# Where prepared weight halves are stored, decoded and fetched in a three-layer chain

## The chip, the cores and the metric

The program runs on one core of a Trainium2 chip, in one launch. The metric is the device time of that core in microseconds (us), lower is better; three runs of the kernel before gave a median of 1521.45 us (1521.2 to 1522.31). The profile shows one execution of its own, which took 1519.77 us, of which the span from its first to its last instruction is 1518.0 us.

The engines named below: PE (TensorE) multiplies matrices, DVE (VectorE), ACT (ScalarE) and POOL (GpSimd) work element by element, and SP (SyncE) issues every DMA of this program from one queue. Each engine executes its own list of instructions in the order in which it was written; between engines there are only waits on semaphores.

## The reference, cut to what matters

```python
attn_out = attention(q, k, v)            # 2 x 8 heads x 768 tokens x 64, state decays per head
x = attn_out.transpose(0, 2, 1, 3).reshape(1536, 512)
# mixture of 8 experts, every token goes through all of them
P = sinkhorn(exp(x @ w_gate - max))      # 8 rounds, 1536 x 8
for e in range(8):                       # w1[e] 512 x 1024, w2[e] 1024 x 512
    out += P[:, e:e+1] * (maximum(x @ w1[e], 0) @ w2[e])
x = out
# a last layer with 2048 hidden columns and float64 weights
h = x @ w_in
out = (maximum(h, 0) + alpha * minimum(h, 0)) @ w_out
```

All three layers are wanted to float32 accuracy. The kernel gets it by splitting each operand into a high half that TensorE takes as it is and a low half that holds the rest, and by adding three products (high x high, high x low, low x high).

## The kernel before

After the attention the program is 20 phases in a row (`PHASES`): phases 0 to 7 are the eight experts on the first 768 tokens, phases 8 to 15 the eight experts on the other 768, and phases 16 to 19 the last layer, two for each half of the tokens. Each phase has a first layer and a second layer.

**First layer.** It is done by blocks: `order` (L1000 to L1003) lists 28 block products, four column blocks j = 0 to 3 with seven products p = 1 to 7 each, and `product` (L606) issues six matmuls of 384 columns for each. The bookkeeping that joins the products is in `after` (L654): after product 1, ACT copies the bank A into the bank B (L669), and PE needs that copy before product 6 may add to B. After product 5, ACT copies D into d. After product 6, DVE writes E = B + d (L672), and after product 7 it writes D = B + d (L685); both must have read B before PE adds the next product to it. `block` turns the finished banks into the high and low halves of the hidden layer (`hh` by ACT, `hl` by DVE).

**Second layer, phases 0 to 7.** `layer2` (L697) goes through six token pieces t; in one piece PE does 24 matmuls of 512 columns, in two halves, keys `t0a` and `t0`, up to `t5a` and `t5`. After each piece DVE adds it to `total` (L720). **Second layer, phases 8 to 15.** It is done by blocks again, from halves that were prepared earlier and lie in DRAM (`c2`): `fast2` has 28 steps u = 0 to 27, keys 0 to 27, and `ws_load` (L771) fetches the prepared pieces.

**What is put between.** The table `hooks` holds, for a key, the functions that are called right after the PE work of that key has been written; `at(ph, key, ...)` adds to it, and functions of one key stand in the order in which they were added. So a hook decides after which PE work an instruction stands in the list of its own engine, and nothing else. Four kinds of work are put in by hooks and concern the change:

- *Units of prepared halves.* 32 units (`prep_load`, `prep_sums`, `prep_low`, `prep_store`, L154 to L184) take a block of `w2`, form four sums on DVE (L168), convert them on ACT into the tile `pw` (L170), take the rest on DVE (L177), and store `pw` (1024 KB) to `c2` by SP (L184). The tile `pw` has one buffer: ACT may write the next unit only when the store of the unit before has landed. In phases 1 to 6 there are five units per phase, in phase 7 two.
- *Decoding.* 32 pieces of the float64 weights are read (`rd`), turned into float32 (two DVE steps, one ACT step `ex` at L578, three DVE steps) and stored (`wd`) by `decode` (L572), which then asks for the next `rd`. Phases 1 to 6 take two pieces each, phases 8 to 15 two or three.
- *Token pieces.* 14 pieces of the tokens of the last layer are split by POOL and ACT into the tile `xs` and stored to `xc` (`x_keep`, L228), in phases 9 to 14, and fetched (`x_fetch`) in the second layer of phase 15.
- *Transposes.* `turn` (L849) and `spread_turn` (L837) put a few transposes on PE, with a copy by ACT and a store.

Of the kernel before, what the change touches and what calls it, by code (L numbers as in the profile page):

```python
# [8 lines left out]
F32 = mybir.dt.float32  # L9
# [35 lines left out]
def tile_kernel(ctx, tc, qkT, kv, ctab, w_gate, w1, w2, w_in, w_out, alpha, out):  # L45
# [182 lines left out]
    def x_keep(g, k):  # L228
        b1, b2 = x_load(g, k)
        b11, b12 = b1[:, 0:HT], b1[:, HT:S]  # L230
        b21, b22 = b2[:, 0:HT], b2[:, HT:S]
        ta, tb = (
            tmp.tile([128, 1024], F32, tag="u" + w, name=f"t{w}{g}_{k}")[:, 0:2 * HT].rearrange("p (a b) -> p a b", a=2)
            for w in "ab"
        )
        eng = nc.gpsimd
        src = {B11: b11, T1: ta[:, 0], T2: ta[:, 1], B21: b21, T3: tb[:, 0], B22: b22, T4: tb[:, 1]}
        terms = {T1: (b12, b11), T2: (b22, ta[:, 0]), T3: (b12, b22), T4: (b21, ta[:, 1])}
        held = {}

        def make(q):
# [36 lines left out]
    with tc.manual_schedule():  # L278
# [292 lines left out]

        def decode(u, then):  # L572
            kind, j, half = u
            t = rd.pop(u)
            lo, hi = (t.rearrange("p (f w) -> p f w", w=2)[:, :, q] for q in range(2))
            ex = tp.tile([128, 512], U32, tag="tmp", name=f"ex{kind}_{j}_{half}")
            nc.vector.tensor_scalar(out=ex, in0=hi, scalar1=0x7FF00000, scalar2=None, op0=ALU.bitwise_and)  # L577
            nc.scalar.activation(out=ex, in_=ex, func=AF.Relu, bias=ebias, scale=8.0)  # L578
            a = tp.tile([128, 512], U32, tag="tmp", name=f"a{kind}_{j}_{half}")
            nc.vector.tensor_scalar(  # L580
                out=a, in0=hi, scalar1=0x000FFFFF, scalar2=0x00100000, op0=ALU.bitwise_and, op1=ALU.bitwise_or
            )
            q = a.bitcast(F32)
            nc.vector.scalar_tensor_tensor(out=q, in0=lo, scalar=2.0 ** -32, in1=a, op0=ALU.mult, op1=ALU.add)
            nc.vector.scalar_tensor_tensor(
                out=q, in0=q, scalar=2.0 ** -20, in1=ex.bitcast(F32), op0=ALU.mult, op1=ALU.mult
            )
            nc.vector.scalar_tensor_tensor(
                out=a, in0=hi, scalar=0x80000000, in1=a, op0=ALU.bitwise_and, op1=ALU.bitwise_or
            )  # L590
            nc.sync.dma_start(out=wd[kind][j][:, 512 * half:512 * half + 512], in_=q)
            if then:
                decode_load(then)

# [278 lines left out]
        def decode_at(ph, keys):  # L873
            for key in keys:
                if todo:
                    u = todo.pop(0)
                    at(ph, key, lambda u=u, then=todo[0] if todo else None: decode(u, then))
# [12 lines left out]

        xk = []
        for ph in range(len(PHASES)):
# [25 lines left out]
            if 1 <= ph <= 6:  # L918
                decode_at(ph, ("t0a", "t5a"))
                prep_at(ph, (0, 2), (1, 1))  # L920
                for t in range(1, 5):
                    prep_at(ph, f"t{t}a", f"t{t}")
            elif ph == 7:
                prep_at(ph, (0, 2), (1, 1))
                prep_at(ph, (1, 2), (2, 1))
            elif fast:
                decode_at(ph, ((0, 6), (2, 5)) if ph % 2 else ((0, 6), (1, 1), (2, 5)))
                if ph > E + 1:
# [39 lines left out]
        for a, (key, later) in enumerate((("t3", (0, 1)), ("t4", (0, 1)), ("t4", (0, 5)), ("t5", (0, 5)))):  # L968
# [3 lines left out]
        at(1, (0, 7), spread_turn)  # L972
        for a in range(KD):
# [25 lines left out]

        order = [(0, 1), (0, 5), (0, 6), (0, 2), (0, 7)]  # L1000
        for j in range(1, NJ):
            order += [(j, 1), (j, 5), (j - 1, 4), (j, 6), (j - 1, 3), (j, 2), (j, 7)]
        order += [(NJ - 1, 3), (NJ - 1, 4)]  # L1003
        for ph in range(len(PHASES)):
# [93 lines left out]
```

## Time and profile before

| | |
|---|---|
| median of three runs | 1521.45 us |
| the profiled execution | 1519.77 us, span 1518.0 us |
| PE busy | 1329.6 us (88%), 7179 matmuls |
| DVE, ACT, POOL busy | 938.1, 631.9, 401.2 us |
| DMA | 296.79 MB, 58.0% of the 16 engines' time |
| mean granted clock of TensorE | 0.940 |

A busy PE is not a PE at its best: matmuls are pipelined, and the profile also counts those that run at the lower of the two clock levels. So the table is read with the length of each phase beside it: the phases from 1 on take between 60 and 100 us, for nearly the same number of matmuls.

### The profile page before, as it was taken

To read this page: it belongs to the slowest core of one execution; us is meant where nothing else is said; L and a number is where in the kernel's file an instruction comes from. 1 tells how busy PE (TensorE), PEld (TensorE's weight loads), DVE (VectorE), ACT (ScalarE), POOL (GpSimd) and SP (SyncE) were. 2 spreads that over 40 slices of the span, in tenths; PEclk is the share of its full clock that TensorE was granted. 3 is DMA by queue.
4 is the path that set the end of the run, shared out by engine and by line. 5 is a ranking of instruction groups with operands and counts; after the bars stand their busy time and mean duration, and the time that the engine had idled before them with its cause. 6 is when DMAs were issued, how large, how long until landed. Compare 5 with 4: busy or idle time off the path is not lost.

```text
span 1518.0 us, 19409 instructions
## 1 busy us (share of the span) xinstructions
PE 1329.6 (88%) x7179; PEld 1229.0 (81%) x7179; DVE 938.1 (62%) x1562; ACT 631.9 (42%) x1129; POOL 401.2 (26%) x335
## 2 busy tenths in 40 slices
PE   9899959687795949659898989988898999999998
PEld 6798849586785849558797979988798998898897
DVE  5666655655555646546576757867577786377552
ACT  2544324241423324234444444634445454364551
POOL 3843203040312204031001212030320227153440
PEclk9999979899897979879999989999999999999999
DMA  9453857567484856647575747675675756132211
GB/s 367 142 194 124 278 195 239 197 210 261 161 298 153 276 202 215 207 156 229 200 265 186 263 142 265 199 261 193 215 231 166 264 212 216 62 112 83 98 42 42
DMA packets 123070, 296.79 MB, mean 196 GB/s; under 512 B 11440, under 2 KB 43744, under 8 KB 118880
## 3 DMA queue, kind: packets, MB, share of 16 engines
q1 hardware_dynamic: 122976, 295.56, 58.0%
q8 instruction: 56, 0.92, 0.2%
q14 instruction: 38, 0.31, 0.1%
HBM read 198.24 MB, written 97.28 MB: 195 GB/s over the span
## 4 chain that ended last, share of the span: by engine, by line
PE 55%; DMA 20%; DVE 10%; ACT 7%; issue 4%; POOL 2%; SPq 1%; ACTq 0%; DVEq 0%
DMA c<-pw 11%; PE B L187 6%; PE B L188 6%; PE B L189 6%; PE o L187 5%; PE o L189 5%; PE o L188 5%; PE A L187 3%; PE A L189 3%; PE A L188 3%; DMA xc<-xs 3%; PE E L187 2%; PE E L188 2%; PE E L189 2%; DVE pw L177 2%
## 5 line engine op out<-in xcount | busy, mean ns | idle before, releaser
L113 POOL TENSOR_TENSOR raw<-raw 128x256 f32<-128x256 f32 x108 | 91.0, 853 | 236.0 <-DVE raw L113 91.1
L170 ACT ACTIVATE pw<-pr 128x1024 fp32r<-128x1024 f32 x32 | 33.9, 1058 | 266.7 <-DMA c<-pw 210.7
L762 DVE TENSOR_TENSOR hs<-b,hs 128x768 fp32r<-128x768 f32 x96 | 93.7, 976 | 52.2 <-ACT hs L761 52.2
L794 POOL TENSOR_TENSOR total<-total,t 128x384 f32<-128x384 f32 x56 | 60.4, 1104 | 237.0 <-DVE t L790 237.0
L761 ACT ACTIVATE hs<-b 128x768 fp32r<-128x768 f32 x96 | 80.9, 843 | 34.0 <-DVE b L736 16.1
L672 DVE TENSOR_TENSOR E<-B,d 128x384 f32<-128x384 f32 x80 | 45.0, 563 | 62.6 <-PE B L189 55.6
L669 ACT ACTIVATE B<-A 128x384 f32<-128x384 f32 x80 | 38.6, 483 | 92.6 <-PE A L189 90.7
L177 DVE TENSOR_TENSOR pw<-pr,pw 128x512 fp32r<-128x512 f32 x64 | 52.6, 863 | 27.9 <-ACT pw L170 27.9
L187 PE MATMUL B<-hs,ws 128*128 128x384 f32 x192 | 64.3, 335 | 2.2 <-DMA ws<-c 2.2
L189 PE MATMUL B<-hs,ws 128*128 128x384 f32 x192 | 64.2, 334 | 0.0
L188 PE MATMUL B<-hs,ws 128*128 128x384 f32 x192 | 64.1, 334 | 0.0
L168 DVE TENSOR_TENSOR pr<-pr 128x256 f32<-128x256 f32 x128 | 57.1, 446 | 4.5 <-DMA pr<-in_w_dram 1.2
L246 POOL TENSOR_TENSOR xs<-b,xs 128x384 fp32r<-128x384 f32 x6 | 7.1, 1188 | 174.3 <-ACT xs L245 174.3
L720 DVE SCALAR_TENSOR_TENSOR total<-o,P,total 128x512 f32<-128x512 f32 x42 | 31.4, 747 | 27.6 <-PE o L189 27.6
L578 ACT ACTIVATE ex<-ex,ebias 128x512 uint32<-128x512 uint32 x32 | 23.2, 724 | 58.6 <-DVE ex L577 58.6
L685 DVE TENSOR_TENSOR D<-B,d 128x384 f32<-128x384 f32 x48 | 27.1, 565 | 31.9 <-PE B L189 31.9
L628 DVE SCALAR_TENSOR_TENSOR hl<-D,hh 128x384 fp32r<-128x384 f32 x32 | 17.8, 557 | 43.8 <-ACT hh L627 41.6
L113 DVE TENSOR_TENSOR raw<-raw 128x256 f32<-128x256 f32 x84 | 44.0, 541 | 1.4
L187 PE MATMUL A<-hs,ws 128*128 128x384 f32 x128 | 42.9, 335 | 0.0
L188 PE MATMUL A<-hs,ws 128*128 128x384 f32 x128 | 42.8, 335 | 0.0
L189 PE MATMUL A<-hs,ws 128*128 128x384 f32 x128 | 42.8, 334 | 0.0
L714 ACT ACTIVATE total<-o 128x512 f32<-128x512 f32 x18 | 10.8, 598 | 69.7 <-PE o L189 69.7
(3435 smaller groups left out, 4745.3 us busy)
## 6 DMA issues: line engine op xcount, KB each, us to landing
ws<-c SPq DMA_DIRECT2D x112, 512.0 KB, 6.0
raw<-in_w_dram SPq DMA_DIRECT2D x64, 512.0 KB, 4.1
c<-pw SPq DMA_DIRECT2D x32, 1024.0 KB, 6.0
c<-raw SPq DMA_DIRECT2D x32, 512.0 KB, 5.2
pr<-in_w_dram SPq DMA_DIRECT2D x32, 512.0 KB, 6.9
raw<-c SPq DMA_DIRECT2D x32, 512.0 KB, 6.3
raw<-wd SPq DMA_DIRECT2D x32, 512.0 KB, 3.6
raw<-in_w_dram SPq DMA_DIRECT2D x32, 384.0 KB, 5.2
```

Source lines behind the costliest of these rows:

```text
L113: eng.tensor_tensor(out=out, in0=in0, in1=in1, op=op)
L168: nc.vector.tensor_tensor(out=out, in0=in0, in1=in1, op=op)
L170: nc.scalar.activation(out=ph2[i][:, :, 0, :], in_=pr[i].rearrange("p (a b) -> p a b", a=4), func=AF.Copy)
L177: nc.vector.tensor_tensor(out=ph2[i][:, a:a + 2, 1, :], in0=v[:, a:a + 2], in1=ph2[i][:, a:a + 2, 0, :].bitcast(F32), op=ALU.subtract,)
L187: nc.tensor.matmul(ps, ah, bh, start=first, stop=False, skip_group_check=True)
L188: nc.tensor.matmul(ps, ah, bl, start=False, stop=False, skip_group_check=True)
L189: nc.tensor.matmul(ps, alo, bh, start=False, stop=last, skip_group_check=True)
L669: nc.scalar.activation(out=banks[n, "B"], in_=banks[n, "A"], func=AF.Copy)
L672: nc.vector.tensor_tensor(out=banks[n, "E"], in0=banks[n, "B"], in1=banks[n, "d"], op=add)
L761: nc.scalar.activation(out=hi, in_=src, func=AF.Copy)
L762: nc.vector.tensor_tensor(out=lo, in0=src, in1=hi.bitcast(F32), op=ALU.subtract)
L794: nc.gpsimd.tensor_tensor(out=dst, in0=dst, in1=tt[m, h], op=ALU.add)
```

## The change

It changes hooks, and cuts `decode` and `x_keep` into steps that can hang on different keys; the arithmetic is the same.

- The list `order` is built earlier in the code, unchanged, so that keys can be taken from it by number.
- `prep_at` takes three keys. Before, the store of a unit stood at the start of the next unit, in front of that unit's load, sums and conversion. Now each unit has a key for its own store. The five units of phases 1 to 6 stood at (0, 2) and at `t1a` to `t4a`; they now start at (0, 2), (2, 5), `t0a`, `t2a` and `t4a`, with low halves at (1, 1), (2, 6), `t0`, `t2`, `t4`, and stores at (1, 6), (2, 7), `t1a`, `t3a`, `t5a`. Phase 7 has the first two.
- `decode` is cut into `bits`, `power` and `join`. In phases 1 to 6 there are three pieces per phase, whole, at `t1a`, `t3a`, `t5a`, where two stood at `t0a` and `t5a`. In phases 8 to 14 there are two pieces each, their steps on three keys of the first layer.
- `x_keep` gives four steps (term, high half, low half, store), `xs` has two buffers, and two of three units of a phase stand in the second layer, at steps 9 to 17 and 18 to 27.
- The fetches of phase 15 stand at 14 steps from 1 to 27 instead of 0 to 13; two of the transposes of phase 8 move from (0, 1) and (0, 5) on to (3, 5) and (3, 6), and `spread_turn` in phase 1 from (0, 7) to (3, 5).

```diff
-        def prep_at(ph, k1, k2):
+        def prep_at(ph, k1, k2, k3):
...
-            at(ph, k1, lambda: prep_store(i - 1), lambda: prep_load(i + 1), lambda: prep_sums(i))
+            at(ph, k1, lambda: prep_load(i + 1), lambda: prep_sums(i))
             at(ph, k2, lambda: prep_low(i))
-            if i == NJ * E - 1:
-                at(ph, (3, 7), lambda: prep_store(i))
+            at(ph, k3, lambda: prep_store(i))
...
             if 1 <= ph <= 6:
-                decode_at(ph, ("t0a", "t5a"))
-                prep_at(ph, (0, 2), (1, 1))
-                for t in range(1, 5):
-                    prep_at(ph, f"t{t}a", f"t{t}")
+                for t in (1, 3, 5):
+                    decode_at(ph, f"t{t}a", f"t{t}a", f"t{t}a")
+                prep_at(ph, (0, 2), (1, 1), (1, 6))
+                prep_at(ph, (2, 5), (2, 6), (2, 7))
+                for t in (0, 2, 4):
+                    prep_at(ph, f"t{t}a", f"t{t}", f"t{t + 1}a")
             elif ph == 7:
-                prep_at(ph, (0, 2), (1, 1))
-                prep_at(ph, (1, 2), (2, 1))
+                prep_at(ph, (0, 2), (1, 1), (1, 6))
+                prep_at(ph, (2, 5), (2, 6), (2, 7))
             elif fast:
-                decode_at(ph, ((0, 6), (2, 5)) if ph % 2 else ((0, 6), (1, 1), (2, 5)))
+                for q in ((6, 8, 9), (13, 15, 16)) if ph == E else ((4, 6, 7), (12, 14, 15)):
+                    decode_at(ph, *(order[i] for i in q))
...
                 if E < ph < 2 * E - 1:
-                    for k1, k2 in (((1, 2), (2, 1)), ((2, 6), (3, 1)), ((3, 5), (3, 3))):
+                    for keys in (((2, 1), (2, 2), (2, 7), (3, 4)), (9, 11, 13, 17), (18, 20, 22, 27)):
...
-            t = held[q] = pools["fast"].tile([128, 2, HT], F32R, tag="xs", name=f"xs{g}_{k}_{q}")
+            t = held[q] = pools["fast"].tile([128, 2, HT], F32R, tag="xs", bufs=2, name=f"xs{g}_{k}_{q}")
```

The first place is SP's queue in the second layer of phase 3, from the copy of the first weights of phase 4 (`c_16`) on. Before, the store of a unit (`c<-pw`) stands just ahead of the load for a later one (`pr`):

```order
L126 DMA c_16_96<-raw_16_2970 128x1024
L184 DMA c_2_114<-pw_2897 128x2048
L158 DMA pr_3259<-in_w_dram 128x1024
L149 DMA c_3_115<-v15h 128x2x256
L150 DMA c_3_115<-v15h 128x256
L149 DMA c_3_115<-v15l 128x2x256
L150 DMA c_3_115<-v15l 128x256
L91 DMA raw_18_3292<-in_w_dram 128x1024
L184 DMA c_2_114<-pw_3265 128x2048
```

Now, at the same place:

```order
L126 DMA c_16_96<-raw_16_2993 128x1024
L606 DMA wd_3_125<-a_3_0_3293 128x512
L574 DMA rd_3_1_3300<-in_w_in_dram 128x1024
L183 DMA c_3_115<-pw_3248 128x2048
L149 DMA c_3_115<-v15h 128x2x256
L150 DMA c_3_115<-v15h 128x256
L149 DMA c_3_115<-v15l 128x2x256
L150 DMA c_3_115<-v15l 128x256
L91 DMA raw_18_3328<-in_w_dram 128x1024
L158 DMA pr_3343<-in_w_dram 128x1024
```

The store of the unit now stands behind the store and the load of a decoded piece (`wd`, `rd`), since the hook of the decoding is added first, and the `pr` load stands behind `raw_18`.

The second place is DVE's list in the first layer of phase 3, around the block j = 2. Before:

```order
L98 TENSOR_TENSOR v12l<-raw_12_2484,v12h 128x1024
L672 TENSOR_TENSOR E_3042<-B_3009,d_3025 128x384
L628 SCALAR_TENSOR_TENSOR hl_10_3034<-B_2921,hh_10_3033 128x384
L628 SCALAR_TENSOR_TENSOR hl_01_3052<-E_2954,hh_01_3051 128x384
L98 TENSOR_TENSOR v13l<-raw_13_2534,v13h 128x1024
L685 TENSOR_TENSOR D_3018<-B_3009,d_3025 128x384
```

Now:

```order
L98 TENSOR_TENSOR v12l<-raw_12_2507,v12h 128x1024
L168 TENSOR_TENSOR pr_2913<-pr_2913 128x256 x4
L689 TENSOR_TENSOR E_3073<-B_3032,d_3048 128x384
L645 SCALAR_TENSOR_TENSOR hl_10_3065<-B_2943,hh_10_3064 128x384
L177 TENSOR_TENSOR pw_3056<-pr_2913,pw_3056 128x2x256 x2
L645 SCALAR_TENSOR_TENSOR hl_01_3085<-E_2976,hh_01_3084 128x384
L98 TENSOR_TENSOR v13l<-raw_13_2557,v13h 128x1024
L702 TENSOR_TENSOR D_3041<-B_3032,d_3048 128x384
```

Four sums stand ahead of E, and two low halves, which wait for ACT's conversion, stand ahead of D.

The third place is ACT's list in phase 9, where the splits of the token pieces (`xs`) stand among the copies that PE waits for. Before:

```order
L761 ACTIVATE hs_2_6819<-b_9_6644 128x768
L669 ACTIVATE B_6829<-A_6822 128x384
L664 ACTIVATE d_6840<-D_6833 128x384
L245 ACTIVATE xs_0_5_6843<-ta_0_6608 128x384
L683 ACTIVATE b_9_6852<-B_6746 128x384
```

Now the same piece stands in the second layer:

```order
L778 ACTIVATE hs_13_7162<-b_9_6897 128x768
L97 ACTIVATE wc41h<-raw_41_6846 128x768
L246 ACTIVATE xs_0_5_7187<-ta_0_6663 128x384
L97 ACTIVATE wb41h<-raw_41_6846 128x512
L686 ACTIVATE B_7263<-A_7256 128x384
```

The split has left the first layer, where the next copies for PE stood right behind it.

## Rows read from the trace of the kernel before

**Rows 1.** Who waited for whom: us in total, times, longest.
```profile
ACT pw L170 <- DMA c<-pw: 210.7, 27, 13.4
...
PE B L187 <- ACT B L669: 124.6, 13, 15.3
...
PE B L187 <- DVE E L672: 35.0, 14, 4.9
...
ACT xs L245 <- DMA xc<-xs: 22.8, 6, 5.1
```

**Rows 2.** By stretches: phases 1 to 6; 7; 8 to 10; 11; 12 to 15; 16.
```profile
core 0: us, PE busy (x) PEld busy (x) DVE busy (x) ACT busy (x) POOL busy (x), PEclk, DMA share, GB/s
128.92:626.27 497.35, 397.47 (x1876) 358.29 (x1875) 287.60 (x501) 169.17 (x285) 122.77 (x96) 0.89 0.65 221
626.27:726.09 99.82, 69.99 (x326) 62.55 (x324) 52.40 (x89) 35.57 (x64) 17.48 (x12) 0.85 0.55 185
726.09:935.04 208.95, 188.39 (x1024) 185.07 (x1022) 143.20 (x202) 96.77 (x169) 25.42 (x23) 0.94 0.67 220
935.04:995.00 59.96, 58.90 (x338) 58.26 (x337) 45.27 (x64) 31.17 (x53) 9.64 (x10) 1.00 0.69 227
995.00:1263.95 268.95, 243.70 (x1345) 238.87 (x1345) 191.31 (x266) 125.97 (x217) 55.79 (x52) 0.97 0.67 223
1263.95:1326.29 62.34, 62.27 (x314) 56.07 (x313) 32.77 (x59) 31.53 (x57) 30.98 (x26) 1.00 0.32 102
```

**Rows 3.** Timeline of PE, phases 2 and 3: start, duration, [idle before <- releaser].
```profile
226.50 0.65 PE L187 MATMUL B<-xh,wc9h 128*128 128x384 f32 x1 [3.47 <-ACT B L669]
...
230.25 0.34 PE L187 MATMUL A<-xh,wa9h 128*128 128x384 f32 x1
...
242.00 0.44 PE L187 MATMUL B<-xh,wb10h 128*128 128x384 f32 x1
...
249.39 0.39 PE L187 MATMUL o<-v8h,hh 128*128 128x512 f32 x1
...
298.66 0.69 PE L187 MATMUL B<-xh,wc12h 128*128 128x384 f32 x1 [14.37 <-ACT B L669]
...
311.68 0.69 PE L187 MATMUL B<-xh,wc13h 128*128 128x384 f32 x1 [5.12 <-ACT B L669]
```

**Rows 4.** Timeline of ACT, phases 2 and 3, the conversions of three units.
```profile
275.82 1.06 ACT L170 ACTIVATE pw<-pr 128x1024 fp32r<-128x1024 f32 x1 [8.15 <-DMA c<-pw]
...
294.75 1.06 ACT L170 ACTIVATE pw<-pr 128x1024 fp32r<-128x1024 f32 x1 [8.14 <-DMA c<-pw]
...
309.08 1.06 ACT L170 ACTIVATE pw<-pr 128x1024 fp32r<-128x1024 f32 x1 [5.66 <-DMA c<-pw]
```

**Rows 5.** Timeline of DVE, second layer of phase 2.
```profile
255.04 0.75 DVE L720 SCALAR_TENSOR_TENSOR total<-o,P,total 128x512 f32<-128x512 f32 x1 [1.45 <-PE o L189]
...
257.90 1.79 DVE L168 TENSOR_TENSOR pr<-pr 128x256 f32<-128x256 f32 x4
...
278.04 1.29 DVE L177 TENSOR_TENSOR pw<-pr,pw 128x512 fp32r<-128x512 f32 x2
...
297.05 0.42 DVE L577 TENSOR_SCALAR ex<-rd 128x512 uint32<-128x512 uint32 x1
```

**Rows 6.** Timeline of SP's queue, start of phase 3.
```profile
300.09 0.33 SPq L591 DMA_DIRECT2D wd<-a  x1
...
301.48 0.38 SPq L184 DMA_DIRECT2D c<-pw  x1
```

**Rows 7.** The tile `pw`: its 32 stores, from issue to landing.
```profile
DMA to landing us min/median/max: 4.8/6.0/8.6
```

**Rows 8.** Timeline of DVE, first layer of phases 2 and 3.
```profile
240.24 1.23 DVE L98 TENSOR_TENSOR v9l<-raw,v9h 128x1024 fp32r<-128x1024 f32 x1 [1.43 <-ACT v9h L97]
...
241.39 0.56 DVE L685 TENSOR_TENSOR D<-B,d 128x384 f32<-128x384 f32 x1
...
311.03 2.91 DVE L177 TENSOR_TENSOR pw<-pr,pw 128x512 fp32r<-128x512 f32 x2
```

**Rows 9.** Timeline of ACT, phase 9.
```profile
826.03 0.52 ACT L245 ACTIVATE xs<-ta 128x384 fp32r<-128x384 f32 x1 [4.76 <-DMA xc<-xs]
```

More of the change, by code (lines that the diff above doesn't have):

```diff
@@ L249, in store @@
             nc.sync.dma_start(out=xc[:, q, :, k, :], in_=held[q].bitcast(F32))
-        return [(lambda q=q: make(q), lambda q=q: store(q)) for q in (B11, T1, T2, B21, T3, T4, B22)]
+        return [[lambda q=q, fn=fn: fn(q) for fn in (term, high, low, store)] for q in (B11, T1, T2, B21, T3, T4, B22)]
     def x_fetch(g, q, w):
@@ L570, in decode_load, with decode_steps @@
             nc.sync.dma_start(out=rd[u], in_=(w_in, w_out)[kind][j][:, 1024 * half:1024 * half + 1024])
-        def decode(u, then):
+        def decode_steps(u, then):
             kind, j, half = u
[L574 to L593, printed above, removed]
@@ new lines, in decode_steps, with bits @@
+            held = {}
+            def bits():
+                t = held["t"] = rd.pop(u)
+                lo, hi = (t.rearrange("p (f w) -> p f w", w=2)[:, :, q] for q in range(2))
+                ex = held["ex"] = tp.tile([128, 512], U32, tag="tmp", name=f"ex{kind}_{j}_{half}")
+                nc.vector.tensor_scalar(out=ex, in0=hi, scalar1=0x7FF00000, scalar2=None, op0=ALU.bitwise_and)
+                a = held["a"] = tp.tile([128, 512], U32, tag="tmp", name=f"a{kind}_{j}_{half}")
+                nc.vector.tensor_scalar(
+                    out=a, in0=hi, scalar1=0x000FFFFF, scalar2=0x00100000, op0=ALU.bitwise_and, op1=ALU.bitwise_or
+                )
+                nc.vector.scalar_tensor_tensor(
+                    out=a.bitcast(F32), in0=lo, scalar=2.0 ** -32, in1=a, op0=ALU.mult, op1=ALU.add
+                )
@@ new lines, in power, with join @@
+            def power():
+                nc.scalar.activation(out=held["ex"], in_=held["ex"], func=AF.Relu, bias=ebias, scale=8.0)
+            def join():
+                t, a, ex = (held[q] for q in ("t", "a", "ex"))
+                hi = t.rearrange("p (f w) -> p f w", w=2)[:, :, 1]
+                q = a.bitcast(F32)
+                nc.vector.scalar_tensor_tensor(
+                    out=q, in0=q, scalar=2.0 ** -20, in1=ex.bitcast(F32), op0=ALU.mult, op1=ALU.mult
+                )
+                nc.vector.scalar_tensor_tensor(
+                    out=a, in0=hi, scalar=0x80000000, in1=a, op0=ALU.bitwise_and, op1=ALU.bitwise_or
+                )
+                nc.sync.dma_start(out=wd[kind][j][:, 512 * half:512 * half + 512], in_=q)
+                if then:
+                    decode_load(then)
@@ L868, in tile_kernel @@
         pool, dve = nc.gpsimd, nc.vector
+        order = [(0, 1), (0, 5), (0, 6), (0, 2), (0, 7)]
+        for j in range(1, NJ):
+            order += [(j, 1), (j, 5), (j - 1, 4), (j, 6), (j - 1, 3), (j, 2), (j, 7)]
+        order += [(NJ - 1, 3), (NJ - 1, 4)]
         todo = []
@@ L871, in tile_kernel, with decode_at @@
             todo += [(k, NJ * ee + j, half) for k in range(2) for j in range(NJ) for half in range(2)]
[L873 to L877, printed above, removed]
+        def decode_at(ph, *keys):
+            if todo:
+                u = todo.pop(0)
+                for key, fn in zip(keys, decode_steps(u, todo[0] if todo else None)):
+                    at(ph, key, fn)
         unit = [0]
-        def prep_at(ph, k1, k2):
+        def prep_at(ph, k1, k2, k3):
             i = unit[0]
@@ L949, in tile_kernel @@
                         unit[0] += 1
-                        at(ph, k1, lambda i=i: xk[i][0]())
-                        at(ph, k2, lambda i=i: xk[i][1]())
+                        for q, key in enumerate(keys):
+                            at(ph, key, lambda i=i, q=q: xk[i][q]())
             if ph + 1 in XGROUP:
@@ L955, in tile_kernel @@
                     at(ph, 0, lambda: new_x(2))
-                    for i, q in enumerate((B11, T1, T2, B21, T3, T4, B22)):
-                        for w in range(2):
-                            at(ph, 2 * i + w, lambda q=q, w=w: x_fetch(2, q, w))
+                    for i, u in enumerate((1, 4, 7, 10, 13, 15, 16, 18, 19, 21, 22, 24, 25, 27)):
+                        q = (B11, T1, T2, B21, T3, T4, B22)[i // 2]
+                        at(ph, u, lambda q=q, w=i % 2: x_fetch(2, q, w))
                     continue
@@ L967, in tile_kernel @@
             at(E, ((0, 7), (1, 5), (1, 6), (1, 2), (2, 1), (2, 6))[w], lambda w=w: ws_load(E, w))
-        for a, (key, later) in enumerate((("t3", (0, 1)), ("t4", (0, 1)), ("t4", (0, 5)), ("t5", (0, 5)))):
+        for a, (key, later) in enumerate(zip(("t3", "t4", "t4", "t5"), (order[i] for i in (0, 1, 20, 22)))):
             at(E - 1, key, lambda a=a: turn(2, a, 0))
@@ L998, in do @@
                 fn()
[L1000 to L1003, printed above, removed]
         for ph in range(len(PHASES)):
```

11 lines of the change are left out of this document (7 added, 4 removed).

## The prediction

> **What bounds the kernel now.** The list of waits comes first. PE waits 124.6 us in 13 places for ACT's copy of the bank B, and 35.0 us in 14 places for DVE's E; ACT itself waits 210.7 us in 27 places for the store of `pw` [rows 1]. The reader is to see a chain: ACT may not convert a unit before the last unit's store has landed, and whatever stands behind the conversion on ACT waits along, the copy of B at the next phase's start included.
>
> Second, the table by phases. Phase 16 has the work of a slow phase without units and decoding and takes 62.34 us at a granted clock of 1.00; phases 1 to 6 take 497.35 us together and phase 7 takes 99.82, at 0.89 and 0.85. Phase 11 has decoding and no stall, 59.96 us, while its neighbours take 208.95 us (three phases) and 268.95 us (four) [rows 2]. So unstalled phases would leave 497.35 - 6 x 62.3 = 123 us in phases 1 to 6, 37 in phase 7 and 477.9 - 7 x 59.96 = 58 in the fast ones: 218 us at most.
>
> Third, the timeline at the start of phase 3. The second layer of phase 2 begins at T = 249.39. PE stops for 14.37 us until 298.66 and again for 5.12 us until 311.68 [rows 3]; so it stood ready at 284.3 (T+34.9), and at 306.6, 7.9 us after the first resumption. ACT's conversions start at 294.75 and 309.08, both released by the store's landing [rows 4], and PE goes on 3.91 and 2.60 us later.
>
> **The change part by part.** *The units in the second layer.* Three units stand there instead of four, and the store goes out before the next unit. But it stands behind a decoded piece's `wd` and `rd` in SP's queue, and `wd` waits for the last decoding step on DVE. I follow the chain from T:
>
> 1. DVE's first `total` starts at T+5.65 as before; sums and the low half of the next weights follow, so DVE is free at 257.90, T+8.5 [rows 5]. Low half of the unit: 1.2 us (of 1.29, the next starts a little before its end), T+9.7. Decoding: from `ex` at 297.05 [rows 5] to `wd` at 300.09 [rows 6], 3.04 us: T+12.75. `wd` and `rd` take SP some 0.8 us: the store is asked for at T+13.55.
> 2. Landing. The trace has 4.8 to 8.6 us [rows 7]. The nearest is the store at 301.48 with `wd`, `rd` and a 512 KB store of raw weights ahead of it, until 309.08: 7.6 us [rows 4, 6]. Without the last I take 7.0. The second conversion starts at T+20.55, although its sums are long done.
> 3. From a conversion to its low half: 278.04 - 275.82 = 2.22 us [rows 4, 5], then 1.2, 3.04 and 0.8: the next store at T+27.8, landed at T+34.8. The third conversion starts then, and PE's copy of B is ready 3.91 later: T+38.7. PE stands ready at T+34.9. **First wait: about 4 us** instead of 14.
> 4. The last store is asked for 301.48 - 298.66 = 2.8 us after PE resumes, less about 0.5 for the raw store that no longer stands ahead: 2.3. With 7.0 for landing and 2.6 to the copy, PE may go on 11.9 us after it resumed, and is ready after 7.9: **second wait 4.0 us**, which is hardly better than the 5.12 of before.
>
> *The unit in the first layer.* At (2, 5) its store before is asked for well ahead, so the landing costs nothing unless it takes over 8 us. But DVE's list is full there: D starts at 241.39 and PE's product that needs it starts at 242.00, as soon as D is done [rows 3, 8]. The sums and low halves are put ahead of it. I take 2.3 us for the sums (1.79 alone), 1.5 for the low half (1.29 alone), and 1.1 for the conversion in between, less the 1.43 that DVE idles there: **3.5 us, a new wait of PE**, part of it already at E. Bounds: 0 (if the idle time takes more) and 6 us (low halves took 2.91 at 311.03 [rows 8], sums stretched alike to 4).
>
> A rule speaks here against the change: the Trainium skill, page "SBUF — State Buffer", section "Who interferes with whom", says that a DVE instruction with two SBUF inputs is shut out while a GpSimd instruction reads SBUF. The 2.91 against 1.29 us of the same instruction agrees [rows 5, 8]. By it alone the wait would be the upper bound, and the time some 17 us longer.
>
> *The clock.* After the 3.47 us wait at 226.50 matmuls take 0.65 us instead of 0.34, until 230.25 [rows 3]. Four half products fill these 3.75 us; at the pace of phase 16 (62.34 us with 28 products and six pieces, about 1.04 us a product) they take 2.1. So a wait of this size costs 1.7 us more. Two of them, 3.4 us; for the third, which falls into two short pieces, I charge nothing (bounds 0 and 1.7).
>
> A slow phase becomes 62.3 + 4.0 + 4.0 + 3.5 + 3.4 = 77.2 us. Phase 1 has no store ahead of it, 62.3 + 3.5 = 65.8. Phases 1 to 6: 65.8 + 5 x 77.2 = 451.8, a gain of 45.5. Phase 7 loses its unit at (1, 2), with nothing in its place that waits; with 2 us for its transposes (an estimate) 79.2, a gain of 20.6.
>
> *The fast phases.* The waits for E come from whole pieces of decoding (3 us of DVE at one place) and from `xs`: ACT waits 22.8 us for `xc<-xs` [rows 1], 4.76 of it at 826.03 [rows 9], with PE's copies behind. After the change no phase has more than two pieces, in steps, and `xs` has two buffers, two units in three in the second layer. Phase 11 shows that two whole pieces and no `xs` cost nothing. I take 1 us above it for each of the other seven: 477.9 - 7 x 60.96 = 51.2 us. Bounds: 58, and 0 if the stalls move along into the second layer, where the splits meet DVE's work on `hs`.
>
> *Edits at nothing.* The fetches of phase 15 land under its 28 steps; phase 16 wants the last piece some 9 products after its start, which hides 9 us; without that cover it costs one landing, some 8.6 us at most [rows 7]. The transposes are the same instructions elsewhere. One more decoded piece per slow phase is 3.04 us of DVE in the second layer, and stands in the chain above.
>
> Sum: 45.5 + 20.6 + 51.2 = 117.3; 1519.77 - 117.3 = 1402.5. The median of the runs shown is 1.7 us above the profiled execution: **1404 us**.
>
> **The rivals.** *Landing decides less.* At 4.8 us to land, the store is there 2.2 us sooner each time: the first wait is 0 and the second 2.9, with one clock loss, so a slow phase takes 62.3 + 2.9 + 3.5 + 1.7 = 70.4. Six phases give 41 us more, 1363; without the DVE wait as well another 24, 1339. For it: stores with no decoded piece ahead land in 6.0 (median). Against: each store of the second layer has `rd` ahead.
>
> *Landing and DVE at their worst.* At 8.6 us the waits are 7.1 and 5.6, and the third is 6: 84.4 us, about the old length; with phase 1 the slow phases give back 46: 1450.
>
> *The fast phases gain nothing*, because POOL's splits slow DVE's `hs` in the second layer: 1404 + 51 = 1455. For it, DVE is busy 45 of 60 us even in phase 11; against, PE's waits named are all in the first layer.
>
> *Slower than before: the stores choke.* The bytes of a slow phase go through in a shorter phase, 221 GB/s [rows 2] would become about 240, and each store of the second layer stands behind 768 KB more. Per phase each further us of landing costs 2 in the first wait, 1 in the second and, past 8 us, 1 at (2, 5). From about 12 us the gain is gone, fast phases included; at 13 it is 1404 + 6 phases x 4 x 6 = 1548 us. Against: the longest landing seen is 8.6 [rows 7].
>
> *The change doesn't do what it says* is half true in the forecast: the store is not asked for at once in the second layer, but after a decoded piece.
>
> **How the numbers follow.** The forecast 0.47 (own range 1375 to 1432, from the DVE wait's bounds and half a us of landing); the shorter landing 0.27; the worst 0.12; the fast phases' failure 0.10; slower 0.04. From 1350 to 1455 leaves out the far ends of the second and the last. What this measurement can tell from no change is about 0.2%, 3 us; beyond it on the faster side lies nearly all: faster 0.95, same 0.02, slower 0.03.
>
> **What would show it.** In the profile after, PE's waits for ACT's B should fall from 124.6 to some 45 us, in 12 places of which half are about 4 us; ACT's waits for `c<-pw` should stay above 50 us, after stores that follow `rd` in SP's queue. PE should wait for DVE's D or E near (2, 7) and (2, 4) of phases 1 to 7. Phases 2 to 6 should take about 77 us each, 8 to 15 about 61. Wrong it is if the first wait is gone, if no wait at D appears, or if the fast phases stay near 68.

## The result and the profile after

The changed kernel takes 1416.52 us (median of four, 1405.09 to 1420.47) against 1521.88 us for the kernel before on the same chip: a ratio of 0.9294, with an interval from 0.9247 to 0.9341. The profiled execution is the 1405.09 us one, span 1403.4 us, mean granted clock 0.974 (0.940 before). The working behind the forecast ended at 1402.5 us for a profiled execution, 2.6 us under this one; the forecast of 1404 is 12 us under the median.

The table by stretches, phases 1 to 6; 7; 8 to 10; 11; 12 to 15; 16, which answers to [rows 2]:

```profile
core 0: us, PE busy (x) PEld busy (x) DVE busy (x) ACT busy (x) POOL busy (x), PEclk, DMA share, GB/s
128.76:593.09 464.33, 398.03 (x1877) 356.71 (x1876) 315.53 (x539) 173.38 (x294) 128.12 (x96) 0.94 0.73 249
593.09:673.21 80.12, 68.11 (x326) 61.01 (x324) 47.33 (x82) 33.03 (x61) 17.19 (x12) 0.94 0.65 223
673.21:855.56 182.35, 178.30 (x1023) 176.05 (x1022) 139.17 (x192) 97.14 (x167) 26.82 (x22) 1.00 0.73 238
855.56:914.13 58.57, 58.57 (x337) 58.27 (x337) 44.85 (x64) 31.46 (x53) 11.34 (x11) 1.00 0.77 246
914.13:1149.03 234.90, 234.13 (x1345) 233.20 (x1345) 179.66 (x246) 125.54 (x213) 56.83 (x52) 1.00 0.70 234
1149.03:1211.51 62.48, 62.43 (x313) 56.00 (x313) 32.72 (x59) 31.53 (x57) 30.95 (x26) 1.00 0.38 133
```

Phases 1 to 6 gave back 33.0 us, phase 7 19.7 and the fast phases 8 to 15 together 62.0 (537.86 before, 182.35 + 58.57 + 234.90 = 475.82 now). That is the whole difference of the two profiled executions, 114.7 us. In the fast phases PE now hardly idles (470.99 of 475.82 us busy). Phases 2 to 7 still take 16 to 18 us more each than phase 16.

The list of waits, which answers to [rows 1] (us in total, times, longest):

```profile
ACT pw L170 <- DMA c<-pw: 133.5, 18, 10.8
...
PE B L186 <- ACT B L686: 53.6, 13, 7.1
...
PE B L186 <- DVE D L702: 17.3, 8, 2.6
...
PE B L186 <- DVE E L689: 11.5, 12, 2.6
```

PE's waits for ACT's B fell from 124.6 to 53.6 us but did not go, and ACT still waits 133.5 us for stores of `pw`. PE's waits for DVE's D, 1.3 us in two places before, are now 17.3 us in eight. ACT's wait for `xc<-xs` is no longer in the list. PE's timeline, from the start of the second layer of phase 2 (T = 246.13) on and through phase 3, to be held against [rows 3], shows where the three waits stand:

```profile
246.13 0.39 PE L186 MATMUL o<-v8h,hh 128*128 128x512 f32 x1
...
285.80 0.69 PE L186 MATMUL B<-xh,wc12h 128*128 128x384 f32 x1 [4.77 <-ACT B L686]
...
297.43 0.69 PE L186 MATMUL B<-xh,wc13h 128*128 128x384 f32 x1 [3.75 <-ACT B L686]
...
311.28 0.44 PE L186 MATMUL B<-xh,wc14h 128*128 128x384 f32 x1 [0.87 <-DVE E L689]
...
317.29 0.44 PE L186 MATMUL B<-xh,wb14h 128*128 128x384 f32 x1 [2.60 <-DVE D L702]
```

The first wait was 14.37 us, the second 5.12. Behind the first, the stretch from 285.80 on ran at a granted clock of 0.61:

```profile
285.80:289.60 3.80, 3.80 (x14) 3.80 (x15) 3.31 (x7) 0.41 (x2) 0.00 (x0) 0.61 0.46 100
```

SP's queue (start, time to issue) and ACT's conversions (in brackets the idle time and its releaser) over the same second layer, beside [rows 4, 6], give the chain:

```profile
258.88 0.32 SPq L606 DMA_DIRECT2D wd<-a  x1
259.24 0.43 SPq L574 DMA_DIRECT2D rd<-in_w_in_dram  x1
260.10 0.32 SPq L183 DMA_DIRECT2D c<-pw  x1
...
274.94 0.41 SPq L183 DMA_DIRECT2D c<-pw  x1
...
288.03 0.45 SPq L183 DMA_DIRECT2D c<-pw  x1
```

```profile
266.82 1.06 ACT L170 ACTIVATE pw<-pr 128x1024 fp32r<-128x1024 f32 x1 [8.54 <-DMA c<-pw]
...
281.84 1.06 ACT L170 ACTIVATE pw<-pr 128x1024 fp32r<-128x1024 f32 x1 [9.10 <-DMA c<-pw]
...
294.84 1.06 ACT L170 ACTIVATE pw<-pr 128x1024 fp32r<-128x1024 f32 x1 [4.27 <-DMA c<-pw]
```

Each store goes out right behind `wd` and `rd`, and each conversion starts when it has landed, 6.7, 6.9 and 6.8 us later. PE goes on 3.96 and 2.59 us after the second and the third conversion.

DVE in the first layer of phase 2, the place of the new wait, beside [rows 8]:

```profile
230.39 1.79 DVE L168 TENSOR_TENSOR pr<-pr 128x256 f32<-128x256 f32 x4
232.10 0.56 DVE L689 TENSOR_TENSOR E<-B,d 128x384 f32<-128x384 f32 x1
...
233.73 0.56 DVE L645 SCALAR_TENSOR_TENSOR hl<-B,hh 128x384 fp32r<-128x384 f32 x1 [1.08 <-ACT hh L644]
234.21 2.38 DVE L177 TENSOR_TENSOR pw<-pr,pw 128x512 fp32r<-128x512 f32 x2
...
238.11 0.55 DVE L702 TENSOR_TENSOR D<-B,d 128x384 f32<-128x384 f32 x1
```

The four sums hold E up; D is held up by the two low halves and by the conversion ahead of them, behind which ACT's `hh` and so DVE's `hl` stand. PE waited 0.86 us at 232.71 and 2.60 us at 238.72. POOL beside it:

```profile
227.54 1.84 POOL L98 TENSOR_TENSOR wc11l<-raw,wc11h 128x768 fp32r<-128x768 f32 x1 [0.56 <-ACT wc11h L97]
234.68 1.37 POOL L98 TENSOR_TENSOR wb11l<-raw,wb11h 128x512 fp32r<-128x512 f32 x1 [5.29 <-ACT wb11h L97]
```

It was idle while the sums ran and at work during the low halves, which took 2.38 us instead of 1.29 [rows 5].

### The profile page after: what moved, and what is told of

It reads as the page before. It is cut to its first block, busy times and chain, and to the rows that moved or that the text cites. A ratio compares the mean times of both kernels' runs of the same rounds, so it can differ in the third digit from the quotient of the medians.

```text
span 1403.4 us, 19428 instructions
## 1 busy us (share of the span) xinstructions
PE 1309.8 (93%) x7179; PEld 1211.8 (86%) x7179; DVE 944.8 (67%) x1562; ACT 633.9 (45%) x1129; POOL 410.3 (29%) x335
## 4 chain that ended last, share of the span: by engine, by line
PE 62%; DVE 13%; DMA 11%; ACT 6%; issue 4%; SPq 2%; POOL 1%; ACTq 0%; DVEq 0%
PE B L186 7%; DMA c<-pw 7%; PE B L188 7%; PE B L187 7%; PE o L186 5%; PE o L188 5%; PE o L187 5%; PE A L186 4%; PE A L187 4%; PE A L188 4%; DVE pw L177 3%; PE E L188 2%; PE E L186 2%; PE E L187 2%; PE D L188 2%
## 5 line engine op out<-in xcount | busy, mean ns | idle before, releaser
L113 POOL TENSOR_TENSOR raw<-raw 128x256 f32<-128x256 f32 x108 | 94.8, 888 | 234.9 <-DMA raw<-in_w_dram 73.7
L779 DVE TENSOR_TENSOR hs<-b,hs 128x768 fp32r<-128x768 f32 x96 | 97.4, 1015 | 30.9 <-ACT hs L778 30.9
L170 ACT ACTIVATE pw<-pr 128x1024 fp32r<-128x1024 f32 x32 | 33.9, 1059 | 173.7 <-DMA c<-pw 133.5
L689 DVE TENSOR_TENSOR E<-B,d 128x384 f32<-128x384 f32 x80 | 45.1, 563 | 58.1 <-PE B L188 53.6
L177 DVE TENSOR_TENSOR pw<-pr,pw 128x512 fp32r<-128x512 f32 x64 | 59.2, 967 | 25.8 <-ACT pw L170 25.8
L731 ACT ACTIVATE total<-o 128x512 f32<-128x512 f32 x18 | 10.8, 598 | 69.0 <-PE o L188 69.0
L113 DVE TENSOR_TENSOR raw<-raw 128x256 f32<-128x256 f32 x84 | 36.9, 457 | 1.4
```

The costliest lines, as they stand in the source:

```text
L113: eng.tensor_tensor(out=out, in0=in0, in1=in1, op=op)
L170: nc.scalar.activation(out=ph2[i][:, :, 0, :], in_=pr[i].rearrange("p (a b) -> p a b", a=4), func=AF.Copy)
L177: nc.vector.tensor_tensor(out=ph2[i][:, a:a + 2, 1, :], in0=v[:, a:a + 2], in1=ph2[i][:, a:a + 2, 0, :].bitcast(F32), op=ALU.subtract,)
L689: nc.vector.tensor_tensor(out=banks[n, "E"], in0=banks[n, "B"], in1=banks[n, "d"], op=add)
L779: nc.vector.tensor_tensor(out=lo, in0=src, in1=hi.bitcast(F32), op=ALU.subtract)
```

## The experiments

Ten kernels, in three groups; in each, the kernel before ran on the same chip (medians 1528.04, 1526.42 and 1522.58 us). All are edits of the changed kernel. The lengths of the phases in their profiled executions, in us:

| kernel | median | ratio to before | phases 1-6 | 7 | 8-15 |
|---|---|---|---|---|---|
| before | 1521.88 | 1 | 497.35 | 99.82 | 537.86 |
| changed | 1416.52 | 0.9294 [0.9247, 0.9341] | 464.33 | 80.12 | 475.82 |
| again | 1408.20 | 0.9227 [0.9195, 0.9259] | 464.65 | 79.93 | 475.19 |
| store_first | 1343.65 | 0.8797 [0.8783, 0.8810] | 409.78 | 68.57 | 478.90 |
| early_only | 1469.99 | 0.9651 [0.9619, 0.9683] | 511.14 | 95.69 | 476.54 |
| late_store | 1508.71 | 0.9877 [0.9862, 0.9892] | 549.32 | 93.53 | 478.05 |
| unit_later | 1417.22 | 0.9277 [0.9263, 0.9291] | 470.49 | 82.35 | 479.04 |
| both | 1333.08 | 0.8738 [0.8714, 0.8762] | 403.75 | 66.31 | 476.87 |
| both_after_copy | 1339.02 | 0.8770 [0.8749, 0.8790] | 405.62 | 69.12 | 476.40 |
| both_last | 1337.46 | 0.8780 [0.8750, 0.8811] | 404.94 | 69.32 | 476.58 |
| xs_back | 1443.53 | 0.9466 [0.9434, 0.9498] | 466.81 | 80.04 | 510.23 |
| decode_whole | 1416.04 | 0.9269 [0.9253, 0.9285] | 464.06 | 80.10 | 482.26 |

**store_first: the store ahead of the decoded piece.** The units' hooks are added before those of the decoding, so that at one key the store stands first in SP's queue.

```diff
             if 1 <= ph <= 6:
-                for t in (1, 3, 5):
-                    decode_at(ph, f"t{t}a", f"t{t}a", f"t{t}a")
                 prep_at(ph, (0, 2), (1, 1), (1, 6))
                 prep_at(ph, (2, 5), (2, 6), (2, 7))
                 for t in (0, 2, 4):
                     prep_at(ph, f"t{t}a", f"t{t}", f"t{t + 1}a")
+                for t in (1, 3, 5):
+                    decode_at(ph, f"t{t}a", f"t{t}a", f"t{t}a")
```

> The changed kernel with one edit: in phases 1 to 6 the unit's hooks are added ahead of the decoding's, so that the store of a unit stands ahead of wd and rd in SP's queue, and its low half ahead of nothing new. Theory (the store lands late because it is asked for after a decoded piece): the first store of the second layer is asked for at about T+9.7 instead of T+13.6 and has 512 KB less ahead; ACT's conversions then start when their sums are done, PE's waits for ACT's B fall from 53.6 to under 10 us, phases 2 to 7 take about 67 us instead of 79, the time about 1343 us. Rival (landing is set by how much is under way altogether, not by the place in the queue): waits for B stay above 30 us and the time above 1390 us.

Measured: 1343.65 us, as expected. PE's start of the second layer of phase 2 (T = 232.99), SP's queue in it, and the list of waits:

```profile
232.99 0.39 PE L186 MATMUL o<-v8h,hh 128*128 128x512 f32 x1
```

```profile
242.87 0.32 SPq L183 DMA_DIRECT2D c<-pw  x1
...
253.73 0.33 SPq L183 DMA_DIRECT2D c<-pw  x1
...
256.63 0.32 SPq L606 DMA_DIRECT2D wd<-a  x1
257.00 0.43 SPq L574 DMA_DIRECT2D rd<-in_w_in_dram  x1
```

```profile
PE B L186 <- DVE E L689: 19.6, 13, 2.9
PE B L186 <- DVE D L702: 15.9, 8, 2.6
```

The store is asked for 2.9 us ahead of `wd` instead of behind `rd`. PE's waits for ACT's B are gone, the waits for D and E are left (that for E has grown, from 11.5 to 19.6 us in all), and most of ACT's waits ahead of a conversion are now for DVE's sums (65.6 us). Phases 2 to 6 take 67.3 to 68.8 us at a clock of 0.97 to 1.00. So what the changed kernel still lost at the phase starts, some 11 us a phase, came from the decoding steps and the 768 KB ahead of each store. The earlier asking is the larger part: the first store goes out at T + 9.88 instead of T + 13.97, 4.1 us sooner, while the 18 stores of the second layers of phases 1 to 6 land 1.2 us faster (median 5.5 instead of 6.7 us). No run takes away one of the two alone. Between the profiled executions the gain is 63 us (1405.09 to 1342.53), between the medians 73.

**early_only and late_store: the two halves of the change.** In early_only each unit keeps its own early store, but the four units of the second layer stand at their old places; in late_store the units stand at their new places, but each store goes out at the start of the next unit, as before.

```diff
# early_only
-                prep_at(ph, (2, 5), (2, 6), (2, 7))
-                for t in (0, 2, 4):
+                for t in (1, 2, 3, 4):
                     prep_at(ph, f"t{t}a", f"t{t}", f"t{t + 1}a")
# late_store
-            at(ph, k1, lambda: prep_load(i + 1), lambda: prep_sums(i))
+            at(ph, k1, lambda: prep_store(i - 1), lambda: prep_load(i + 1), lambda: prep_sums(i))
             at(ph, k2, lambda: prep_low(i))
-            at(ph, k3, lambda: prep_store(i))
+            if i == NJ * E - 1:
+                at(ph, (3, 7), lambda: prep_store(i))
```

> The changed kernel with the five units of phases 1 to 6 where they stood before, (0, 2) and t1a to t4a, but each with its own early store (keys t2a to t5a); decoding and the rest as changed. Theory (each unit in the second layer needs its landing, some 7 us, and its own 3 to 6 us on DVE and ACT, so four of them don't fit into 32.6 us of PE work, early store or not): the first wait goes from 5 to about 16 us, the waits for D and E at block 2 vanish, phases 2 to 6 take about 87 us, the time about 1450 us. Rival (the early store is all that is needed): no longer than the changed kernel, 1416 us or less.

> The changed kernel with its stores put back to the start of the next unit (ahead of that unit's load and sums, as before the change); places of the units, decoding and everything else as changed. Theory (the early store carries its part of the gain): the stores of the second layer are asked for some 3 us later each, the first wait grows by 3 to 4 us, the second by 1, and at (2, 5) the conversion waits for a store just asked for, so the wait for D grows by 3 to 4 us: 8 us in each of phases 2 to 7, about 1468 us. Rival (fewer units in the second layer do it all): within 10 us of the changed kernel.

Measured: 1469.99 and 1508.71 us. Both expectations had the direction and were too low, by 20 and 41 us. Of early_only, ACT in the second layer of phase 2 and PE behind it:

```profile
274.27 1.06 ACT L170 ACTIVATE pw<-pr 128x1024 fp32r<-128x1024 f32 x1 [9.73 <-DMA c<-pw]
...
288.53 1.06 ACT L170 ACTIVATE pw<-pr 128x1024 fp32r<-128x1024 f32 x1 [9.65 <-DMA c<-pw]
...
299.70 1.06 ACT L170 ACTIVATE pw<-pr 128x1024 fp32r<-128x1024 f32 x1 [8.86 <-DMA c<-pw]
```

```profile
303.60 0.69 PE L186 MATMUL B<-xh,wc12h 128*128 128x384 f32 x1 [19.74 <-ACT B L686]
```

With four units in one second layer the conversions stand 11 to 14 us apart and the last of them runs far into the next phase; the first wait is 18.3 to 19.7 us in phases 2 to 7, where about 16 was expected. Of late_store, SP and ACT at the same place:

```profile
268.29 0.63 SPq L184 DMA_DIRECT2D c<-pw  x1
...
286.42 0.57 SPq L184 DMA_DIRECT2D c<-pw  x1
```

```profile
276.02 1.06 ACT L170 ACTIVATE pw<-pr 128x1024 fp32r<-128x1024 f32 x1 [8.09 <-DMA c<-pw]
...
294.99 1.06 ACT L170 ACTIVATE pw<-pr 128x1024 fp32r<-128x1024 f32 x1 [13.11 <-DMA c<-pw]
```

Each conversion waits for a store that was asked for only at its own hook, so every unit carries a whole landing. In the second layer that makes the first wait 12.4 us on the mean of phases 2 to 7 instead of 5.4; the expectation had 3 to 4 us more, and here lies about half of its miss. In the first layer of phase 3, SP, ACT and the list of waits:

```profile
340.26 0.42 SPq L184 DMA_DIRECT2D c<-pw  x1
```

```profile
346.78 1.06 ACT L170 ACTIVATE pw<-pr 128x1024 fp32r<-128x1024 f32 x1 [8.20 <-DMA c<-pw]
```

```profile
PE D L187 <- DVE hl L646: 31.2, 7, 5.0
```

`hh` stands behind the conversion on ACT, `hl` behind that on DVE, and PE waits 4.39 us for `hl`; such a wait of 4 to 5 us stands in each of phases 1 to 7. The expectation had its size, as 3 to 4 us more at D; the wait for D itself is 2.1 us in phases 2 to 6. In phases 1 to 6 each half alone is slower than the kernel before (511.14 and 549.32 us against 497.35), and of these kernels only the one with both gains there. The third decoded piece per phase stood in both kernels; its price alone was not measured.

**unit_later: the second unit of the first layer moved.** It should take away the wait at D and E.

```diff
-                prep_at(ph, (2, 5), (2, 6), (2, 7))
+                prep_at(ph, (2, 7), (3, 5), (3, 6))
```

> The changed kernel with the second unit of the first layer moved from (2, 5), (2, 6), (2, 7) to (2, 7), (3, 5), (3, 6) in phases 1 to 7, behind the D of block j = 2. Theory (sums and low halves ahead of E and D on DVE make PE's waits of 0.87 and 2.60 us): both waits vanish in seven phases, 24 us and up to 10 us of clock, about 1385 us. Rival (DVE's list is as full at j = 3): the wait reappears at D or E of block 3, and the time is within 8 us of 1416.

Measured: 1417.22 us, no gain that the intervals could tell. The time is as the rival had it, but the wait came back at ACT's copy, not at D or E. PE's waits for D and E shrink to 6.9 us in all, but ACT's B takes their place (73.0 us in 20 places). In phase 3 ACT now converts just ahead of a copy that PE needs, and waits for the sums first; PE waits behind it:

```profile
317.26 1.06 ACT L170 ACTIVATE pw<-pr 128x1024 fp32r<-128x1024 f32 x1 [1.72 <-DVE pr L168]
318.23 0.47 ACT L686 ACTIVATE B<-A 128x384 f32<-128x384 f32 x1
```

```profile
318.75 0.44 PE L186 MATMUL B<-xh,wc15h 128*128 128x384 f32 x1 [2.35 <-ACT B L686]
```

PE waits 2.35 us for that copy, in place of 3.47. In phase 3 the three waits come to 10.2 us instead of 12.0, but the matmuls at the lower rate cost 1.6 us more, behind this wait above all; the phase takes 78.42 us, 78.56 before the edit. Phases 1 to 7 together are 8.4 us longer in the profile than those of the changed kernel: their waits are 4 us shorter, and slower matmuls cost 12 us more. Why the rate falls behind this wait is not shown: in the changed kernel a wait of 2.60 us stands in each of phases 2 to 7 without such a fall. The first wait of phase 2 grows from 7.1 to 8.7.

**both, both_after_copy, both_last: the two edits together, at three places.** store_first, with the second unit at (2, 7), (3, 5), (3, 6); at (3, 1), (3, 6), (3, 2); and at (3, 6), (3, 3), (3, 4).

```diff
# on top of store_first: both; both_after_copy; both_last
-                prep_at(ph, (2, 5), (2, 6), (2, 7))
+                prep_at(ph, (2, 7), (3, 5), (3, 6))
+                prep_at(ph, (3, 1), (3, 6), (3, 2))
+                prep_at(ph, (3, 6), (3, 3), (3, 4))
```

> The two edits together: unit hooks ahead of the decoding in phases 1 to 6, and the second unit of the first layer at (2, 7), (3, 5), (3, 6). If both causes are as the theory has them, phases 1 to 7 come near the 62 to 63 us of phases 16 to 19 and the time is about 1315 us, and repeated runs lie closer together than the 1405 to 1420 us of the changed kernel, since hardly a wait is left after which the clock could fall. If one of them fails, 1340 to 1390 us.

> As the kernel with both edits, but the second unit of the first layer at (3, 1), (3, 6), (3, 2): its conversion then stands behind ACT's copy of B for block 3, not ahead of it. Theory (the 2.04 us wait for that copy is the conversion standing ahead of it, waiting for its sums): the wait goes from six or seven phases, 12 to 14 us, about 1320 us against 1333. Rival (the wait moves on to D or E of block 3): within 5 us of 1333.

> Unit hooks ahead of the decoding in phases 1 to 6, and the second unit of the first layer at (3, 6), (3, 3), (3, 4): its sums stand behind the last E of DVE's list and its low half behind the last D, where nothing of the first layer waits for DVE or ACT any more. Theory (the remaining wait of 2.0 to 2.3 us per phase is one unit ahead of a copy or an add that PE wants): it vanishes in seven phases and nothing takes its place, about 1318 us. Rival (the conversion at t0a, right behind, then waits for a store just asked for, and passes that on to the next phase): 1333 us or more.

Measured: 1333.08, 1339.02 and 1337.46 us, each some 20 us over what was expected. PE's wait of the last block, in phase 3 of both and in phase 4 of the other two, one fence each:

```profile
291.19 0.46 PE L186 MATMUL B<-xh,wc15h 128*128 128x384 f32 x1 [2.04 <-ACT B L686]
```

```profile
363.04 0.45 PE L186 MATMUL B<-xh,wc19h 128*128 128x384 f32 x1 [2.29 <-DVE E L689]
```

```profile
364.52 0.45 PE L186 MATMUL B<-xh,wb19h 128*128 128x384 f32 x1 [1.74 <-DVE D L702]
```

The wait does not go, it changes its name: ACT's B, DVE's E, DVE's D, 1.7 to 2.3 us in each of phases 1 to 7. In the kernel named both they make 14 of the 18 us by which the expectation was missed, and phases 1 to 7 take 65.0 to 68.4 us instead of 62 to 63. Its runs lie closer together than those of the changed kernel, as expected: 1331.69 to 1338.94 us. A unit in the first layer holds up whichever bookkeeping comes next. Over store_first the move to the first of the three places is worth some 10 us (0.8738 against 0.8797, the intervals apart), and among the three places no difference can be told. The version named both is the fastest of all: 195 us under the kernel before on the same chip, and 83 us under the changed one's median.

**xs_back and decode_whole: the fast phases.** In xs_back the token pieces have one buffer and their old, whole places again; in decode_whole the decoded pieces of phases 8 to 14 are whole at (0, 6) and (2, 5).

```diff
# xs_back
-            ... tag="xs", bufs=2, name=f"xs{g}_{k}_{q}")
+            ... tag="xs", name=f"xs{g}_{k}_{q}")
-    for keys in (((2, 1), (2, 2), (2, 7), (3, 4)), (9, 11, 13, 17), (18, 20, 22, 27)):
+    for keys in (((1, 2), (1, 2), (1, 2), (2, 1)), ((2, 6), (2, 6), (2, 6), (3, 1)),
+                 ((3, 5), (3, 5), (3, 5), (3, 3))):
# decode_whole
-    for q in ((6, 8, 9), (13, 15, 16)) if ph == E else ((4, 6, 7), (12, 14, 15)):
-        decode_at(ph, *(order[i] for i in q))
+    for key in ((0, 6), (2, 5)):
+        decode_at(ph, key, key, key)
```

> The changed kernel with the token pieces of phases 9 to 14 as before: one buffer for xs, each piece whole (term, high, low on one key) at (1, 2), (2, 6), (3, 5) and its store at (2, 1), (3, 1), (3, 3). Decoding stays in steps, two pieces per fast phase. Theory (the xs wait on ACT made the 4 us waits of phases 9, 10, 12 and 13): those four phases take 5 to 7 us more, the others nothing, about 1440 us against 1416. Rival (whole decoded pieces on DVE made the stalls of the fast phases): within 8 us of 1416.

> The changed kernel with the decoded pieces of phases 8 to 14 whole on one key, at (0, 6) and (2, 5), two per phase; xs as changed. Theory (with only two pieces, a whole one costs what it cost in phase 11 before, 59.96 us against 58.57 now): 1 to 2 us in each of phases 9 to 14, and some 4 us in phase 8, where the tiles of the transposes are waited for: about 1430 us. Rival (steps were what removed the stalls): 4 us or more in each phase, 1445 us or above.

Measured: 1443.53 and 1416.04 us; beside them, on the same chip, the changed kernel took 1408.20. The list of waits of xs_back:

```profile
ACT xs L246 <- DMA xc<-xs: 28.9, 8, 5.4
...
PE B L186 <- DVE E L689: 23.8, 12, 4.2
```

ACT's wait for the store of `xs` is back, and with it PE's waits for E: the phases 9, 10, 12 and 13 take 66.9 to 68.5 us, 11 and 14 stay at 58.4. In the kernel before, phase 11 has one token piece, which waits for no store:

```profile
948.46 0.52 ACT L245 ACTIVATE xs<-b 128x384 fp32r<-128x384 f32 x1
```

The six waits there stand at the second or third piece of phases 9, 10, 12 and 13. So the token pieces, their second buffer and their new places together, account for 34 of the 62 us (510.23 - 475.82). decode_whole costs 6.4 us in the fast phases (7.1 against `again`), 0.8 to 1.9 us in each of 10 to 14 and nothing in phase 8; its expectation was too high. The other 21 us of the gain came with parts that neither experiment undoes (six decoded pieces that moved out of phases 8 to 15 into phases 1 to 6, the fetches of phase 15, the transposes); they were not told apart. Phases 8 and 15, which neither experiment makes longer by more than 1 us, gained 6.1 and 6.6 us.

**again: the changed kernel once more.** The spread of its runs was wide, 1405 to 1420 us, and the profile was of the fastest.

```diff
+        # same
         order = [(0, 1), (0, 5)
...
```

> The changed kernel itself once more, for a second profile. Its runs lay between 1405 and 1420 us with granted clocks of 0.974 to 0.965, which the kernel before did not do. Theory (the waits are the same in each execution and only the time at the lower clock level after them differs): the profile of an execution near 1416 us shows the same waits of PE within 2 us in sum, and 10 us more lost to slow matmuls. Rival (the stores land later in some executions): PE's waits for ACT's B are 10 us longer than 53.6 us.

Measured: 1408.20 us (1404.61 to 1415.12). The profile was again of the fastest run, 1404.61 us, with phases 1 to 16 the same within 0.8 us and the same waits (PE for ACT's B: 54.2 us). So neither the theory nor the rival, which speak of a slower execution, was put to the test. Over the eight timed runs of the changed kernel and again, time and mean granted clock go together: 0.976 with 1404.6 us, 0.971 with 1415.1, 0.965 with 1420.5. In which stretch the slower runs lose the clock could not be seen.

## Why the prediction was right, and where its terms were off

- **The chain of the second layer** held. From its start T = 246.13 the first store went out at T + 13.97 (predicted 13.55) and the second conversion began at T + 20.69 (20.55). The second store went out at T + 28.81 (27.8); most of the difference is in the decoding, whose two last steps took 1.03 and 1.11 us instead of 0.69. PE was ready at T + 34.9, as predicted, and went on at T + 39.67 (38.7): a wait of 4.77 us instead of "about 4". Over phases 2 to 7 it is 4.3 to 7.1, mean 5.4. The reading that counted was the order in SP's queue, and that order alone was worth 63 us between profiled executions, 73 between medians, as store_first shows.
- **The second wait**, 4.0 predicted: 2.6 to 4.2 us. PE resumed 11.6 us after the first resumption (11.9) and was ready after 7.9 (7.9).
- **The new wait at E and D**, 3.5 predicted: 0.87 + 2.60 = 3.47 us in phases 2 to 7, and in early_only, which has no unit there in phases 1 to 6, it appears in phase 7 alone. The size came out of two errors of opposite sign: the sums were not stretched (1.79 us, I took 2.3), the low halves were (2.38, I took 1.5). The Trainium skill's rule ("SBUF — State Buffer", section "Who interferes with whom"), by which DVE with two SBUF inputs is shut out while GpSimd reads, agrees with these rows: POOL worked for 1.37 us inside the low halves, which took 1.09 us longer than unslowed, and stood idle during the sums; the low halves ended at 236.59, 0.54 us behind POOL's instruction. So the upper bound that I set by it, 6 us (its terms, 4 + 2.91 + 1.1 - 1.43, give 6.6), was not reached.
- **The clock**, 3.4 us a phase: behind the first and the second wait the matmuls at the lower rate cost 3.7 to 4.1 us in phases 2 to 5 and 7 and 2.7 in phase 6, summed over PE's starts against the 0.17 us pace of a 384-column matmul. All that phases 2 to 6 take over 62.3 us and their waits is 4.1 to 4.6 us each, so this term was somewhat small.
- **What was off.** Phase 1 took 69.17 us, 65.8 predicted. In early_only, without the unit at (2, 5), it takes 65.21: the unit adds 4.0 us (3.5 predicted), and the rest is 2.9 us over the yardstick of 62.3 that I had not counted, 2.2 of them waits of 1.37, 0.41 and 0.45 us. Phases 2 to 6 took 395.2 us, 386 predicted: 6.5 us in the first wait (7.1 in phase 2, 4.3 to 5.7 in the others, 4 predicted) and 4.7 in what stands beside the waits, the clock above all, less 1.9 in the second wait. The fast phases gave 62.0 us instead of 51.2: the term was mis-sized since I took phase 11 of before, 59.96 us, as free of stalls and added 1 us to it; with the stalls gone phases 9 to 15 take 58.3 to 60.1, so phase 11 had held 1.4 us of its own. Nor was it a phase without `xs`, as the prediction has it, but one with a single token piece. Whole pieces of decoding, the prediction's other cause, were worth 6.4 us (decode_whole). The two errors, +13.5 and -10.8 us, nearly cancel; that the working ended within 2.6 us of the profiled execution is luck.
- **The rivals.** Landing took 6.7 us (median of the 32 stores), near the 7.0 taken, so the short-landing rival did not come true by itself; store_first goes some way to its condition of 4.8 us (median 5.5 without `rd` ahead, time 1344 us) but does not give its price, since there the store is also asked for 4.1 us sooner. The stores did not choke: 249 GB/s in phases 1 to 6 and 8.0 us for the longest. "Half true" was the right word for what the change says: the store was asked for behind a decoded piece.
- **What the median added.** I carried 1.7 us from a profiled execution to the median; here it was 11.4, within the spread that goes with the clock (0.965 to 0.974).

## What to carry to other kernels

Work out at which place in the issuing queue a store stands, and not only at which step it is asked for: two lines of table code in the other order were worth 63 to 73 us here, where the whole change gave 105 to 115. A tile with one buffer turns the landing of each store into a wait of the engine that fills it, so its units need a distance of one landing plus the work between. A second buffer for `pw`, which would loosen this chain itself, was not tried. A wait that is pushed away from one consumer must be followed to the next: the unit in the first layer cost about 2 us at every one of three places.

## What the runs showed of the hardware that was not expected

- The landing of a 1 MB store went with what was issued just ahead of it more than with the traffic as a whole. In the second layers of phases 1 to 6 it took 6.5 to 7.9 us (median 6.7) just behind `wd` and `rd`, at 249 GB/s in phases 1 to 6, and 3.8 to 7.4 us (median 5.5) ahead of them in store_first, at 288 GB/s. In the first layers of phases 1 to 7 of the changed kernel the first unit's store landed in 3.8 to 4.8 us, the second's, issued in phase 2 right behind two loads of raw weights, in 7.4 to 8.0.
- The mean granted clock of one and the same program differed from run to run, 0.965 to 0.976, and its time with it, by 16 us; the runs of the kernel before spread by 3.6, 4.0, 4.1 and 9.4 us in the four sets.
